# A fused attention and two expert layers in float32: scores of units 8 to 31 from split queries and keys, products with V in one burst

## The chip, the cores and the metric

The kernel runs on one core of a Trainium2 chip. The metric is the device time of one execution in microseconds (us), as the median of several runs. Five engines work side by side, each through its own list of instructions in order: TensorE (PE) for matrix products, VectorE (DVE), ScalarE (ACT), GpSimd (POOL), and SyncE (SP), which here issues nearly all DMAs. PEld is TensorE's loading of the stationary operand.

## The reference

Three layers follow one another: attention with a threshold on the scores, a layer `x -> (h - tanh h) @ w_out`, and a top-1 mixture of eight experts. Only the first is touched.

```python
def _attn_ref(q, k, v, tau):              # (4, 8, 576, 64) each
    scale = 1.0 / np.sqrt(q.shape[-1])
    scores = scale * np.matmul(q, k.transpose(0, 1, 3, 2))
    thresh = np.max(scores, axis=-1, keepdims=True) - tau
    scores = np.where(scores >= thresh, scores, -1000000000.0)
    scores = scores - np.max(scores, axis=-1, keepdims=True)
    attn = np.exp(scores)
    attn = attn / (np.sum(attn, axis=-1, keepdims=True) + 1e-09)
    return np.matmul(attn, v).astype(np.float32)
...
    x = attn_out.transpose(0, 2, 1, 3).reshape(B * S, H * D)      # 2304 x 512
    h = x @ w_in;  x = (h - np.tanh(h)) @ w_out                   # 512 -> 2048 -> 512
    ...                                                           # then top-1 of 8 experts, 512 -> 1024 -> 512
```

## The kernel before

**Stages.** Part A holds attention and, between its instructions, the first steps of the second layer on those chunks of 256 tokens whose attention is done (33 steps in all, `step`: 24 products `ph` of 256 columns at L606 and 12 products `x` of 512 columns at L640 each). Part B does the rest of that layer and the routing, and the last part the experts. Parts B and after are the same before and after the change, and the same 33 steps stand in part A.

**Units.** Attention is cut into 32 units: four batches, two halves of the queries, four pairs of heads (`units`). A unit of the first half has 2 x 128 queries in each of two heads, thus 4 score tiles of 128 queries by 576 keys; one of the second half has 5, the fifth a merged tile with the last 64 queries of both heads. That makes 144 tiles, 16 of them merged.

**A tile's way.** `scores_full` (L948) multiplies queries and keys in plain float32. The contraction over the head's 64 numbers fills half of the array's rows, so the two halves of the keys (288 each) stand on partitions 0 to 63 and 64 to 127 and run as two row tiles side by side: two calls of 288 columns, which the trace shows as four matmuls (`x4`, form 64*128); a merged tile has four calls and eight matmuls (form 64*64). DVE takes the tile out of PSUM with its row minimum of the negated scores (L963, `em`, `mx`), ACT does the exponential (L966, `e`), POOL or ACT the threshold (`tb`), DVE the masked product with the row sum (L976). PE turns the tile in four transposes (`turn`, L1013, `pt`), and ACT copies it to `eth`; the last 64 keys go through L1040 to `elh`.

**Products with V.** `pairs_` (L1058) multiplies by V in plain float32, each head in one half of the array's columns (form 128*64). Its eight calls for key tiles 0 to 3 (`x16` in the trace) are one scheduled piece, its two for key tile 4 (`x4`) a second one. ACT copies the result to `xf`, DVE multiplies by the turned reciprocals (L1097 to L1101), and ACT or POOL round it to `xh` while POOL keeps the remainder `xl`.

**Split numbers.** Elsewhere a float32 number is held as a rounded part (type fp32r) and a remainder (`round_to` at L424 to L428, `rest` at L436 to L444), and a product is made of several passes with these parts. `prep_q`, `prep_k` and the function `scores` hold this form for queries and keys; before, no unit uses them, since `FULL, FULLV = 32, 32`.

**Order.** `Sched` sorts all pieces of parts A and on by a greedy simulation: each piece has an engine, a duration in ns written in the code (for example 700 for `scores_full`, 2200 and 550 for the pieces of `pairs_`), a due time, and buffers with a fixed number of copies. The program is emitted in that order, so a change of such a number reorders all engines.

## Time and profile before

| | before |
|---|---|
| median of 3 runs | 1003.67 us (1002.45 to 1005.86) |
| the profiled execution | 1005.48 us |
| its span, first to last instruction | 1003.7 us |
| granted TensorE clock, mean | 0.996 |
| PE busy | 980.5 us (98%) |
| DVE, ACT, POOL busy | 680.0, 534.6, 316.5 us |
| score matmuls (L954), 640 | 112.2 us |
| products with V (L1062, key tiles 0 to 3), 512 | 70.5 us |

Matmuls are pipelined, so the length of one in the trace holds its way through the array; how much of PE a group takes is read as the distance from its start to the start of the next group, where nothing waits between them. A line `x4` of a timeline is four matmuls in a row.

### The profile page before, as it was taken

To read this page: it belongs to the slowest core of one execution; us is meant where nothing else is said; L and a number is where in the kernel's file an instruction comes from. 1 tells how busy PE (TensorE), PEld (TensorE's weight loads), DVE (VectorE), ACT (ScalarE), POOL (GpSimd) and SP (SyncE) were. 2 spreads that over 40 slices of the span, in tenths; PEclk is the share of its full clock that TensorE was granted. 3 is DMA by queue.
4 is the path that set the end of the run, shared out by engine and by line. 5 is a ranking of instruction groups with operands and counts; after the bars stand their busy time and mean duration, and the time that the engine had idled before them with its cause. 6 is when DMAs were issued, how large, how long until landed. Compare 5 with 4: busy or idle time off the path is not lost.

```text
span 1003.7 us, 18221 instructions
## 1 busy us (share of the span) xinstructions
PE 980.5 (98%) x6559; PEld 785.1 (78%) x6559; DVE 680.0 (68%) x1733; ACT 534.6 (53%) x1130; POOL 316.5 (32%) x531
## 2 busy tenths in 40 slices
PE   6899999999999999999999999999999999999997
PEld 3556677667777767767889888888898988999996
DVE  5988888777667555555268986697556785656640
ACT  4887777777666655656354443444332442334431
POOL 2556665455364434433400110011102320212101
PEclk9999999999999999999999999999999999999999
DMA  5464534644463451442592842321705784556501
GB/s 196 142 230 162 201 121 168 232 150 158 155 221 138 171 186 56 151 162 76 198 357 85 278 153 85 106 105 56 270 22 179 249 271 156 174 165 194 178 5 41
DMA packets 44564, 160.64 MB, mean 160 GB/s; under 512 B 5630, under 2 KB 5630, under 8 KB 38576
## 3 DMA queue, kind: packets, MB, share of 16 engines
q1 hardware_dynamic: 40896, 148.95, 42.7%
q0 software_dynamic: 3424, 10.16, 3.0%
q8 instruction: 54, 0.88, 0.4%
q14 instruction: 46, 0.38, 0.1%
q10 hardware_dynamic: 144, 0.26, 0.1%
HBM read 124.22 MB, written 35.85 MB: 159 GB/s over the span
## 4 chain that ended last, share of the span: by engine, by line
PE 90%; DVE 5%; issue 2%; ACT 1%; POOL 1%; DMA 1%; POOLq 0%; DVEq 0%; ACTq 0%
PE ph L606 21%; PE x L640 20%; PE ph L1615 10%; PE sp L954 8%; PE pv L1062 8%; PE py L1648 7%; PE pt L1013 6%; PE py L1502 4%; DVE em L976 1%; PE ph L1252 1%; DVE em L963 1%; PE pv L1040 1%; PE pt L1547 1%; PE x L700 1%; DMA tau_t<-in_tau_dram 1%
## 5 line engine op out<-in xcount | busy, mean ns | idle before, releaser
L606 PE MATMUL ph<-xh,wi 128*128 128x256 f32 x1152 | 184.9, 289 | 0.2 <-DVE u L629 0.2
L640 PE MATMUL x<-wo,gh 128*128 128x512 f32 x576 | 170.8, 408 | 0.6 <-POOL gh L426 0.6
L606 PEld LDWEIGHTS ph<-xh,wi 128*128 128x128 f32 x1152 | 157.4, 189 | 16.1 <-issue 10.9
L976 DVE SCALAR_TENSOR_TENSOR em<-em,tb,e 128x576 f32<-128x576 f32 x144 | 128.5, 895 | 50.9 <-ACT e L966 26.3
L963 DVE TENSOR_SCALAR_CACHE_REDUCE em<-sp 128x576 f32<-128x576 f32 x144 | 108.5, 754 | 54.7 <-PE sp L954 44.1
L966 ACT ACTIVATE e<-em,mx 128x576 f32<-128x576 f32 x144 | 111.0, 772 | 55.5 <-DVE em L963 47.2
L954 PE MATMUL sp<-kst,qh 64*128 64x288 f32 (+1 forms) x640 | 112.2, 463 | 9.1 <-DMA qh<-in_q_dram 4.9
L640 PEld LDWEIGHTS x<-wo,gh 128*128 128x128 f32 x576 | 98.8, 189 | 24.8 <-issue 9.3
L426 POOL TENSOR_SCALAR gh<-u 128x512 fp32r<-128x512 f32 x52 | 41.4, 797 | 215.8 <-DVE u L629 163.6
L424 ACT ACTIVATE eth<-pt 128x512 f32<-128x512 f32 (+1 forms) x160 | 85.8, 549 | 35.6 <-PE pt L1013 32.9
L606 PE MATMUL ph<-xl,wi 128*128 128x256 f32 x576 | 96.0, 289 | 0.0
L640 PE MATMUL x<-wo,gl 128*128 128x512 f32 x288 | 93.4, 408 | 0.0
L619 ACT ACTIVATE u<-ph 128x512 f32<-128x512 f32 x72 | 42.9, 596 | 94.0 <-PE ph L606 88.0
L1013 PE MATMUL pt<-ident,em 128*128 128x128 f32 x576 | 88.7, 280 | 3.9 <-DVE em L976 3.0
L1013 PEld LDWEIGHTS pt<-ident,em 128*128 128x128 f32 x576 | 67.8, 143 | 26.4 <-issue 8.7
L606 PEld LDWEIGHTS ph<-xl,wi 128*128 128x128 f32 x576 | 79.0, 190 | 6.7 <-issue 6.5
L627 DVE SCALAR_TENSOR_TENSOR w<-w,u 128x512 f32<-128x512 f32 x72 | 50.8, 706 | 45.0 <-ACT w L623 44.9
L954 PEld LDWEIGHTS sp<-kst,qh 64*128 64x128 f32 (+1 forms) x640 | 43.3, 179 | 43.1 <-issue 14.9
L444 DVE TENSOR_TENSOR w<-wraw,w 128x512 fp32r<-128x512 f32 x98 | 66.3, 693 | 11.8 <-ACT w L424 10.4
L1062 PE MATMUL pv<-eth,vt 128*64 128x256 f32 (+1 forms) x512 | 70.5, 417 | 0.0
L1536 POOL DMA_INDIRECT rows<-x2f,gid x20 | 21.9, 1096 | 127.4 <-PE pt L1547 121.2
L974 POOL TENSOR_TENSOR tb<-mx,tau_t 128x1 f32<-128x1 f32 x96 | 32.5, 338 | 91.0 <-DVE em L963 78.2
(372 smaller groups left out, 1807.8 us busy)
## 6 DMA issues: line engine op xcount, KB each, us to landing
wraw<-in_w_dram SPq DMA_DIRECT2D x64, 512.0 KB, 4.2
wi<-wsv SPq DMA_DIRECT2D x17, 1024.0 KB, 4.9
wo<-wsv SPq DMA_DIRECT2D x17, 1024.0 KB, 5.0
craw<-in_w_in_dram SPq DMA_DIRECT2D x14, 512.0 KB, 3.9
craw<-in_w_out_dram SPq DMA_DIRECT2D x14, 512.0 KB, 3.9
kst<-in_k_dram SPq DMA_DIRECT2D x16, 432.0 KB, 4.9
wsv<-wi SPq DMA_DIRECT2D x6, 1024.0 KB, 6.5
wsv<-wo SPq DMA_DIRECT2D x6, 1024.0 KB, 4.5
```

The costliest lines, as they stand in the source:

```text
L424: return sc.add("ACT", act(n, psum), due, lambda: nc.scalar.activation(dst(), src(), AF.Copy), r, w)
L444: return sc.add(eng, dve(n, psum) + 5 if eng == "DVE" else pool_tt(n), due, lambda: e.tensor_tensor(out=dst(), in0=src(), in1=hi().bitcast ...
L606: nc.tensor.matmul(ph.t[:, j, :], wi.t[:, w_, cc * CH + j * P:cc * CH + (j + 1) * P], x_.t[:, cc, :], start=(n == 0 and cc == 0), stop=(n ...
L640: nc.tensor.matmul(x2b[c, half][t].t, g_.t[:, j, t * P:(t + 1) * P], wo.t[:, w_, j * DM:(j + 1) * DM], start=(first and n == 0 and j == 0) ...
L954: nc.tensor.matmul(sp.t[o:o + m_, kb_, 0:KB], qh.t[rows, c0:c0 + m_], kf[rows, j * KB:(j + 1) * KB], start=True, stop=True)
L963: sc.add("DVE", 665, d, lambda ev=ev, sp=sp, mx=mx: nc.vector.tensor_scalar(out=ev().rearrange("p (a b) -> p a b", a=2), in0=sp.t[:, :, 0: ...
L966: sc.add("ACT", 667, d + 800, lambda e=e, ev=ev, mx=mx: nc.scalar.activation(e.t, ev(), AF.Exp, bias=mx.t, scale=-1.0), [(em, h), mx], [e])
L976: sc.add("DVE", 729, d + TAU, lambda ev=ev, tb=tb, e=e, rs=rs, h=h: nc.vector.scalar_tensor_tensor(out=ev(), in0=ev(), scalar=tb.t, in1=e. ...
L1013: nc.tensor.matmul(pt.t[:, kt, :], em.t[:, c0:c0 + P], ident, is_transpose=True, start=(kt == 0), stop=(kt == 3))
L1062: nc.tensor.matmul(pvf()[h * D:(h + 1) * D], vb_.t.rearrange("p a b -> p (a b)")[:, k * D:(k + 1) * D], eth[h].t[:, kt, 0:n] if kt < 4 els ...
L1615: nc.tensor.matmul(ph.t[:, 0:cap], wx()[:, cc * P:(cc + 1) * P], x_.t[:, cc, 0:cap], start=(n == 0 and cc == 0), stop=(n == 2 and cc == 3))
L1648: nc.tensor.matmul(py[j].t[0:size[j]], x_(), wx(), start=(f == 0 and n == 0), stop=(f == 7 and n == 2))
```

## The change

For units 8 to 31 the scores come from split numbers in the full array. `prep_q` loads a unit's queries twice (partitions 0 to 63 and 64 to 127), ACT rounds them to `qh`, and POOL makes the remainder `ql` in two halves. `prep_k` does the same for the keys of a pair of heads: ACT rounds twice 576 columns, and DVE or POOL put the remainder on partitions 64 to 127 (12 pairs of heads, 24 remainders, 12 of them on DVE). A score tile is then four matmuls of 288 columns with 128 contraction rows (rounded keys and remainder stacked, times `qh`, then `ql`); a merged one is ten, six of 288, two of 224 and two of 64 columns. Units 0 to 7 keep `scores_full`. The products with V stay in plain float32, but the ten calls are one piece that waits for `elh` too. The durations written in the code become 880 for `scores_full` and 3080 or 2560 for the burst; a split tile has 528, a merged one 1110. V's tile shrinks from 128 to 64 columns a head and key tile, as half of it was unused.

```diff
-FULL, FULLV = 32, 32
+FULL = 8
...
-        v_ = vts[b, hp] = buf("kv", "vt", 4, [P, 10, P])
-        dma(due - 6000, lambda: nc.sync.dma_start(
-            v_.t.rearrange("p a b -> p (a b)")[:, 0:10 * D],
-            vv[b, hp].rearrange("p a b -> p (a b)")), (), [v_], 327680)
+        v_ = vts[b, hp] = buf("kv", "vt", 4, [P, 10, D])
+        dma(due - 6000, lambda: nc.sync.dma_start(v_.t, vv[b, hp]), (), [v_], 327680)
...
-        full, fullv = ui < FULL, ui < FULLV
+        full = ui < FULL
...
                 if full:
-                    sc.add("PE", 700, d - TAU // 2, scores_full, [qh, kb], [sp])
+                    sc.add("PE", 880, d - TAU // 2, scores_full, [qh, kb], [sp])
                 else:
                     sc.add("PE", 1110 if merged else 528, d - TAU // 2, scores, [qh, ql] + kr_, [sp])
...
-            sc.add("PE", 2200 if half else 1780, dl, lambda: pairs_(range(4)), [vb_] + eth, [pv])
-            sc.add("PE", 550 if half else 445, dl, lambda: pairs_((4,)), [vb_, elh], [pv])
...
+        sc.add("PE", 3080 if half else 2560, dl, lambda: pairs_(range(5)), [vb_, elh] + eth, [pv])
```

The rest of the diff takes out code that no unit reached before (the split form of V's products, `prep_v`, the constant `minus`).

Two places in the order, before and after. First PE in the burst of unit 16 (first half of batch 2), from the last calls of key tiles 0 to 3 on: `sp` are scores, `eth` and `elh` the turned weights of attention, `ph` the second layer. Before:

```order
L1062 MATMUL pv<-eth_2986,vt 64x256
L1062 MATMUL pv<-eth_3011,vt 64x256
L606 MATMUL ph<-xh,wi_2723 128x256 x4
L1062 MATMUL pv<-elh,vt 64x256 x2
L606 MATMUL ph<-xl,wi_2723 128x256 x4
L954 MATMUL sp<-kst,qh 128x288 x2
L606 MATMUL ph<-xh,wi_2723 128x256 x8
```

The same burst after the change:

```order
L1030 MATMUL pv<-eth_3166,vt 64x256
L1030 MATMUL pv<-eth_3229,vt 64x256
L1030 MATMUL pv<-elh,vt 64x256 x2
L928 MATMUL sp<-kst,qh 128x288
L928 MATMUL sp<-kst,ql 128x288
L928 MATMUL sp<-kst,qh 128x288
L928 MATMUL sp<-kst,ql 128x288
L604 MATMUL ph<-xl,wi_2850 128x256 x4
```

Key tile 4 now follows the other four at once, and the score tile is four calls in the array's full form, as the second layer's calls around it are.

Second, POOL while batch 1 is under way, from a masked threshold (`tb`) on. Before:

```order
L974 TENSOR_TENSOR tb<-mx,tau_t 128x1
L995 TENSOR_SCALAR rb<-blk,rs 128x128
L426 TENSOR_SCALAR gh<-u 128x512
L438 TENSOR_TENSOR gl<-u,gh 128x256
L974 TENSOR_TENSOR tb<-mx,tau_t 128x1
L438 TENSOR_TENSOR gl<-u,gh 128x256
```

After:

```order
L959 TENSOR_TENSOR tb<-mx,tau_t 128x1 x2
L980 TENSOR_SCALAR rb<-blk,rs 128x128
L973 TENSOR_SCALAR rs<-rs 128x2
L424 TENSOR_SCALAR gh<-u 128x512
L436 TENSOR_TENSOR gl<-u,gh 128x256 x2
L436 TENSOR_TENSOR kst<-kr,kst 64x288
L424 TENSOR_SCALAR xh<-xf 128x128
L973 TENSOR_SCALAR rs<-rs 128x2
L442 TENSOR_TENSOR xl<-xf,xh 128x128
L436 TENSOR_TENSOR ql<-qr,qh 128x256
```

Remainders of keys (`kst`) and queries (`ql`) now stand among the thresholds, the reciprocals (`rs`) and the second layer's remainders (`gl`).

## Rows read from the trace of the kernel before

**Rows 1.** Busy time in six stretches: length, PE, PEld, DVE, ACT, POOL, clock, DMA.

```profile
25.00:50.00 25.00, 21.83 (x147) 13.05 (x148) 24.76 (x65) 21.14 (x45) 12.62 (x22) 1.00 0.43 143
...
75.00:100.00 25.00, 25.00 (x171) 16.14 (x168) 21.18 (x54) 18.77 (x41) 15.34 (x28) 0.95 0.47 164
100.00:150.00 50.00, 48.76 (x330) 33.65 (x329) 41.38 (x100) 37.15 (x81) 32.09 (x52) 1.00 0.46 162
150.00:200.00 50.00, 50.00 (x348) 34.46 (x347) 40.57 (x98) 36.56 (x79) 26.73 (x50) 1.00 0.59 200
...
450.00:485.00 35.00, 35.00 (x242) 26.08 (x241) 16.75 (x41) 21.79 (x49) 14.52 (x31) 1.00 0.21 76
...
520.00:600.00 80.00, 79.36 (x554) 70.67 (x553) 69.49 (x178) 39.39 (x82) 9.28 (x9) 1.00 0.53 182
```

**Rows 2.** L1062 by itself: duration min/median/max in ns, first and last start.

```profile
L1062 PE MATMUL pv<-elh,vt x128: 379/432/484, 24.3 to 483.3; 128*64 128x256 f32 x64, 128*64 128x320 f32 x64
```

**Rows 3.** PE in order of time around a burst: start, length, line, operation, form.

```profile
220.21 0.64 PE L606 MATMUL ph<-xh,wi 128*128 128x256 f32 x4
220.78 0.76 PE L954 MATMUL sp<-kst,qh 64*128 64x288 f32 x4
221.47 2.37 PE L1062 MATMUL pv<-eth,vt 128*64 128x320 f32 x16
223.67 0.71 PE L1062 MATMUL pv<-elh,vt 128*64 128x320 f32 x4
224.31 0.74 PE L606 MATMUL ph<-xl,wi 128*128 128x256 f32 x4
224.97 0.76 PE L954 MATMUL sp<-kst,qh 64*128 64x288 f32 x4
225.66 0.66 PE L1013 MATMUL pt<-ident,em 128*128 128x128 f32 x4
226.07 1.21 PE L606 MATMUL ph<-xh,wi 128*128 128x256 f32 x8
```

**Rows 4.** PE in order of time around a merged score tile.

```profile
211.88 0.72 PE L954 MATMUL sp<-kst,qh 64*64 64x288 f32 x8
212.53 0.74 PE L606 MATMUL ph<-xh,wi 128*128 128x256 f32 x4
213.10 0.65 PE L606 MATMUL ph<-xl,wi 128*128 128x256 f32 x4
213.58 0.60 PE L1013 MATMUL pt<-ident,em 128*128 128x128 f32 x4
213.94 0.73 PE L606 MATMUL ph<-xh,wi 128*128 128x256 f32 x4
```

**Rows 5.** PE in order of time, unit 16: a burst cut in two.

```profile
235.77 1.95 PE L1062 MATMUL pv<-eth,vt 128*64 128x256 f32 x16
237.65 0.73 PE L606 MATMUL ph<-xh,wi 128*128 128x256 f32 x4
238.31 0.65 PE L1062 MATMUL pv<-elh,vt 128*64 128x256 f32 x4
```

**Rows 6.** PE in order of time in the experts: split products of 288 columns.

```profile
916.89 0.69 PE L1615 MATMUL ph<-xh,w 128*128 128x288 f32 x4
917.42 0.69 PE L1615 MATMUL ph<-xl,w 128*128 128x288 f32 x4
917.95 1.22 PE L1615 MATMUL ph<-xh,w 128*128 128x288 f32 x8
```

**Rows 7.** Groups by line: count, then busy us, mean ns, idle before.

```profile
L424 ACT ACTIVATE wi<-ct 128x512 fp32r<-128x512 f32 x12 | 7.5, 622 | 0.3 <-DVE ct L557 0.3
L444 DVE TENSOR_TENSOR w<-wraw,w 128x512 fp32r<-128x512 f32 x98 | 66.3, 693 | 11.8 <-ACT w L424 10.4
```

**Rows 8.** From 75 to 485 us, single lines: duration min/median/max in ns.

```profile
L438 POOL TENSOR_TENSOR gl<-u,gh x61: 720/738/1297, 76.4 to 484.7; 128x256 fp32r<-128x256 f32 x61
...
L976 DVE SCALAR_TENSOR_TENSOR em<-em,tb,e x118: 800/818/1367, 76.7 to 476.8; 128x576 f32<-128x576 f32 x118
```

More of the change, by code (lines that the diff above doesn't have):

```diff
@@ L345, in tile_main @@
     make_identity(nc, ident)
-    minus = const.tile([P, P], F32R, name="minus")
-    nc.vector.tensor_scalar(out=minus, in0=ident, scalar1=-1.0, scalar2=None, op0=ALU.mult)
     tau_t = const.tile([P, 1], F32, name="tau_t")
@@ L909, in attention @@
         n = 320 if half else 256
-        full, fullv = ui < FULL, ui < FULLV
+        full = ui < FULL
         kb, vb_ = kst[b, hp], vts[b, hp]
         qh, ql = qs
-        dt_ = F32 if fullv else F32R
-        eth = [buf("et", f"eth{h}", 1, [P, 4, 320], dt_) for h in range(2)]
-        elh = buf("et", "elh", 1, [P, 320], dt_)
-        if not fullv:
-            etl = [buf("et", f"etl{h}", 1, [P, 4, 320], F32R) for h in range(2)]
-            ell = buf("et", "ell", 1, [P, 320], F32R)
+        eth = [buf("et", f"eth{h}", 1, [P, 4, 320]) for h in range(2)]
+        elh = buf("et", "elh", 1, [P, 320])
         T0 = k0 * TAU
@@ L1024, in attention @@
                     hi = lambda hh=hh, cols=cols: eth[hh].t[:, :, cols]
-                    if fullv:
-                        round_to("p_h", 4 * wd, d + 400, hi, src, [pt], [(eth[hh], qt)], True)
-                        continue
                     round_to("p_h", 4 * wd, d + 400, hi, src, [pt], [(eth[hh], qt)], True)
-                    lo = lambda hh=hh, cols=cols: etl[hh].t[:, :, cols]
-                    if not merged and pick("p_x") == "Z":
-                        sc.add("PE", 231, d + 700, lambda pt=pt, hi=hi: nc.tensor.matmul(
-                            pt.t, minus, hi(), start=False, stop=True, skip_group_check=True), [(eth[hh], qt)], [pt])
-                        round_to("p_lz", 512, d + 900, lo, src, [pt], [(etl[hh], qt)], True)
-                        continue
-                    rest("p_l", 4 * wd, d + 900, lo, src, hi, [pt, (eth[hh], qt)], [(etl[hh], qt)], True)
             plist.append((em, qt, merged, d))
@@ L1045, in attention @@
             round_to("p_h2", D, dl + 500, lambda: elh.t[D:P, 256:320], lambda: plf()[D:P, 320:384], [pl], [elh], True)
-        if not fullv:
-            rest("p_l", n, dl + 900, lambda: ell.t[:, 0:n], lambda: plf()[:, 0:n], lambda: elh.t[:, 0:n],
-                 [pl, elh], [ell], True)
-        if half and not fullv:
-            rest("p_l", D, dl + 900, lambda: ell.t[D:P, 256:320], lambda: plf()[D:P, 320:384],
-                 lambda: elh.t[D:P, 256:320], [pl, elh], [ell], True)
         xf = buf("ep", "xf", 1, [P, 320])
@@ new lines, in attention, with pairs_ @@
+        pv = buf("ps_v", "pv", 1, [P, 4, P])
+        pvf = lambda: pv.t.rearrange("p a b -> p (a b)")[:, 0:n]
+        def pairs_(kts):
+            for kt in kts:
+                for h in range(2):
+                    k = 2 * kt + h
+                    nc.tensor.matmul(
+                        pvf()[h * D:(h + 1) * D], vb_.t[:, k, :],
+                        eth[h].t[:, kt, 0:n] if kt < 4 else elh.t[:, 0:n], start=(kt == 0), stop=(kt == 4))
+        sc.add("PE", 3080 if half else 2560, dl, lambda: pairs_(range(5)), [vb_, elh] + eth, [pv])
@@ L1151, in tile_main @@
                 raw_k(0, k, (starts[k] - 4) * TAU)
[L1152 to L1153 removed]
+                raw_v(0, k, (starts[k] + 1.5) * TAU)
             qnext = raw_q(0, T0 - 4 * TAU)
@@ L1159, in tile_main @@
             qnext = prep_q(*units[ui + 1], T0 + 0.5 * TAU)
-        if half == 0 and (b or not FULLV):
-            (raw_v if ui < FULLV else prep_v)(b, hp, T0 + 1.5 * TAU)
+        if half == 0 and b:
+            raw_v(b, hp, T0 + 1.5 * TAU)
         if b and half == 0:
@@ L1169, in tile_main @@
             prep_k(b, hp, (starts[ui + 4] - 4) * TAU)
-        if ui < 4 and 0 < FULLV < 8:
-            prep_v(b, hp, (starts[ui + 4] - 2) * TAU)
         sc.kind = "moe"
```

44 lines of the change are left out of this document (2 added, 42 removed), and 3 rows, old and new, of the table ENGINES.

## The prediction

> **What bounds the kernel now.** I read first the table of busy time by stretch. Attention and the second layer's first steps share part A, whose last product with V starts at 483.3 us [rows 2]. From 150 to 200 us PE is busy 50.00 of 50.00 us, from 450 to 485 again 35.00 of 35.00, while DVE is at 0.81 and then 0.48 of the time [rows 1]. Only earlier is it otherwise: from 25 to 50 us DVE is busy 24.76 of 25 and PE 21.83. So in part A, once the second layer can fill the gaps, the end is set by how much PE has to do; every us taken from PE's list there moves all that follows, until DVE or ACT come up to it. The clock is full in these stretches but one (0.95 from 75 to 100 us) [rows 1].
>
> A busy PE says nothing of how long its pieces are, so I next read PE's list in order of time, by the distance from a group's start to the next group's start. In [rows 3] a plain score tile takes 221.47 - 220.78 = 0.69 us. The `ph` group ahead of it takes 220.78 - 220.21 = 0.57, where a `ph` group with split products on both sides, or transposes behind it, takes 213.58 - 213.10 = 0.48 [rows 4]: going over from the full array to row or column tiles costs 0.09. The `ph` group behind a score tile takes 213.10 - 212.53 = 0.57 [rows 4], so the way back costs 0.09 too. Both are paid at one group in 224.97 - 224.31 = 0.66, which comes from column tiles and goes to row tiles [rows 3]. These changes are a hidden half of the cost of the scores: a tile between full-array work costs 0.69 + 0.09 + 0.09 = 0.87.
>
> **The change part by part.**
>
> *The ordinary score tile of units 8 to 31* (96 tiles): 0.69 before. After, it is four split matmuls of 288 columns in the full array, and the experts run just these: four in 917.42 - 916.89 = 0.53 us, weights loaded anew for each [rows 6]. Saved: 96 x 0.16 = 15.4 us.
>
> *The merged tile* (12 of them): before, 212.53 - 211.88 = 0.65 [rows 4]. After, six matmuls of 288 columns at 0.53/4 = 0.13 make 0.80, and two of 224 at no more than 0.48/4 = 0.12 [rows 4] make 0.24, rather 0.21 as they have fewer columns. For those of 64 columns no row exists; their price lies between 64/288 of 0.13, which is 0.03, and the 0.10 that one transpose of 128 columns takes, 226.07 - 225.66 = 0.41 for four behind a score tile [rows 3]. I take 0.10, as the transpose too has 128 weight columns to load. Sum 1.21, lost: 12 x 0.56 = 6.7 us (at the lower end 5.0).
>
> *The changes of form.* I counted them in the order of the two programs, up to the end of attention: from full array to tiles 138 times before and 54 after, back 139 and 55, directly between scores' row tiles and V's column tiles 51 and 11. Saved: 84 pairs at 0.09 + 0.08 (some of the ways back lead to transposes, which pay only 0.06: 0.41 for four behind a score tile [rows 3] against 213.94 - 213.58 = 0.36 behind `ph` [rows 4]) = 14.3 us; and 40 direct changes at something between 0 and 0.10, for which I take 0.07, 2.8 us. In this count lies the burst's part: before, 15 of the 32 bursts are cut in two by other work, as in [rows 5], where `ph` stands between and takes 238.31 - 237.65 = 0.66 with both changes in it; after, none is. The burst's own calls stay as they are (2.20 and 0.64 us in [rows 3]). It now waits for `elh` as well; behind it wait PE's next scores, and DVE for these, but in 17 of 32 bursts the second piece followed directly before, so that `elh` was there in time. I cost that wait at nothing while the second layer's steps stand ahead of the burst; without that cover it is at most the 0.4 us or so of one copy, for 15 bursts 6 us, which I keep for the range.
>
> *Sum on PE:* 15.4 - 6.7 + 14.3 + 2.8 = 25.8 us less.
>
> *What other engines get.* ACT: 24 roundings of queries (512 or 704 columns) and 24 of keys (576), at 622 ns for 512 columns [rows 7] some 0.62 to 0.8 each: 33 us. POOL: 48 half remainders of queries and 24 of keys; 256 columns take 738 ns [rows 8], 352 in proportion 1.0: 61 us. DVE: 12 remainders at 0.70 [rows 7], 8 us. They are off PE's path as long as they come half a unit early; in the order the second half of `ql` stands at least some hundred allocations ahead of its first score, where a unit has about two hundred. SP issues 36 more DMAs, for the halves that are loaded twice; bytes hardly change, and transfers have a share of 0.46 to 0.59 [rows 1]. The load is nevertheless near the top for a stretch: from 100 to 200 us DVE was busy 82 of 100 us, ACT 74, POOL 59 [rows 1]. With PE's work there some 9 us shorter and a fifth of the added work in it, DVE comes to 0.92, ACT to 0.88, POOL to about 0.8.
>
> *What that costs PE* no row shows for this mix, so I bound it. Below: nothing, as from 150 to 200 us with DVE at 0.81. Above: 3.17 of 25 us, or 13%, as from 25 to 50 us with DVE at 0.99 and little to fill the gaps. Between lie 1.24 of 50 us, 2.5% (100 to 150 us, DVE 0.83), and 0.64 of 80 us, 0.8%, with DVE at 0.87 and ample split products [rows 1]. I take 2.5% for the first 100 us of the changed part and 0.8% for the other 285: 2.5 + 2.3 = 4.8 us.
>
> *A rule that speaks against this.* DVE's masked product takes 818 ns in the middle and 1367 at most, POOL's remainder 738 and 1297 [rows 8]: now and then one stands still for about the length of the other, mostly not. The Trainium skill (SBUF — State Buffer, SBUF: two separate sides) calls the port pair of VectorE and GpSimd an exclusive lock, held for the whole instruction, for VectorE's instructions with two inputs from SBUF among others. The longest durations here agree with that; the medians, 18 ns above the shortest, say that it strikes seldom. By the rows it is thus a few us in DVE's gaps and nothing in the sum; what it would be if it struck each time is the last rival.
>
> *Total:* 25.8 - 4.8 = 21.0 us less. The profiled execution of before took 1005.48 us with a span of 1003.7, so it would be 984.5 there; it lies 1.8 above the median of 1003.67, against which I forecast **982.7 us**.
>
> **The rivals.**
>
> *DVE and ACT take over until batch 2.* For: DVE at 0.92, and in-order engines lose at each late input; PE's planned durations now are near the true ones, which leaves others less slack. Against: units 8 to 12 had filled gaps at 0.83, and the second layer's steps lie several units behind, so PE has other work. Price: 13% on the first 100 us and 2.5% on the rest, 13 + 7.1 = 20.1; 25.8 - 20.1 = 5.7 less, 998 us.
>
> *The split queries come late: slower.* Each unit's first tile needs the load, one rounding on ACT and two remainders on POOL, with POOL's list of thresholds and `gl` ahead of them, and only two copies of `ql`. If PE stood still for a whole conversion at each of 24 units, 0.7 + 2 x 0.87 = 2.4 us, that is 58 us against 25.8 saved: 1036 us. It decides from 25.8/24 = 1.1 us per unit on. For: POOL would have to be at about 0.8. Against: the order places it half a unit ahead, some 7 us.
>
> *The forms change as before.* If the split tiles between transposes (plain float32) pay as much at each change as row tiles do, the 17.1 us for changes are not had: 25.8 - 17.1 - 4.8 = 3.9 less, 999.8 us. Against: `ph` groups stand between transposes and split products all over part A, and in [rows 4] a change from `ph` to transposes takes nothing (0.48).
>
> *DVE and POOL stop each other: slower.* If each of the 72 new POOL operations kept a DVE operation waiting for its whole length, as the longest of [rows 8] do, and each such wait reached PE, that would be 61 us against 25.8: 1039 us. It decides from 25.8/72 = 0.36 us each on. Against: the medians of [rows 8], and DVE's idle 18 of each 100 us from 100 to 200. This is the lock of the page named above, taken at its word.
>
> **How the numbers follow.** Forecast, 976 to 991 us (25.8 with the merged tile at its lower end and no idle, down to 13 less where `elh` and the port cost 8): 0.71. Better than that: 0.03. DVE and ACT, 991 to 1000: 0.14. The forms: 0.05. Late queries: 0.05. The port: 0.02. The range of 975 to 995 takes in the forecast and half of the first rival, with 0.2 left out. About 0.3%, 3 us, is what a measurement of this kernel can tell from no change. Faster by more: 0.88; within it 0.05, the weak ends of the two milder rivals; slower 0.07.
>
> **What would show it.** Right: a split tile takes 0.53 to the next start, the `ph` group ahead of it 0.48; the last product with V starts some 20 us earlier than 483.3; PE's idle time between 75 us and that point stays under 8 us, and the parts behind keep their length. The first rival shows as PE idle on DVE's row minimum or masked product between 100 and 220 us; the second as PE's scores waiting for POOL's `ql` or `kst`; the third as split tiles of 0.7. The forecast is wrong if PE's list isn't the bound once it is shorter, or if part B doesn't start earlier by what part A saves.

## The result, and the profile after

The changed kernel takes **995.21 us** (median of four runs, 992.77 to 995.42), beside 1004.32 us for the kernel before (1002.45 to 1005.86): a ratio of 0.9905, 95% interval 0.9881 to 0.9928. That is faster by 9.1 us where 21.0 were forecast, and just outside the range, whose upper end was 995.

| | before | after |
|---|---|---|
| profiled execution, its span | 1005.48, 1003.7 us | 995.42, 993.5 us |
| mean granted clock | 0.996 | 0.995 |
| PE busy | 980.5 us | 960.0 us |
| DVE, ACT, POOL busy | 680.0, 534.6, 316.5 us | 710.5, 559.2, 400.8 us |
| V burst of unit 7 starts | 105.49 us | 117.27 us |
| V burst of unit 31 starts | 480.84 us | 472.87 us |

First the table of busy time by stretch (length, PE, PEld, DVE, ACT, POOL, clock, DMA), the rows that answer to [rows 1] and the stretch from 50 to 75 us beside them:

```profile
25.00:50.00 25.00, 19.97 (x125) 11.52 (x123) 21.89 (x56) 17.98 (x37) 9.86 (x20) 0.93 0.37 126
50.00:75.00 25.00, 20.40 (x134) 12.94 (x136) 21.45 (x52) 18.47 (x39) 14.23 (x22) 0.93 0.63 206
75.00:100.00 25.00, 23.29 (x157) 14.52 (x153) 23.24 (x51) 21.01 (x45) 18.39 (x31) 1.00 0.53 165
100.00:150.00 50.00, 45.92 (x333) 35.16 (x333) 46.58 (x107) 40.08 (x88) 42.84 (x63) 1.00 0.60 187
150.00:200.00 50.00, 50.00 (x366) 41.85 (x365) 46.83 (x105) 42.29 (x93) 43.26 (x64) 1.00 0.51 171
200.00:300.00 100.00, 98.95 (x714) 83.75 (x714) 85.02 (x183) 78.45 (x170) 81.13 (x120) 1.00 0.58 183
450.00:485.00 35.00, 35.00 (x241) 29.29 (x240) 14.92 (x44) 17.66 (x43) 15.95 (x30) 1.00 0.33 118
```

From 150 us on PE is as full as before, with one us missing from 200 to 300. What is new stands above that: from 25 to 150 us PE is idle 5.03 + 4.60 + 1.71 + 4.08 = 15.4 us. Before it was 3.17 + 0 + 1.24 by [rows 1], and 2.34 more by the row of before that was not shown:

```profile
50.00:75.00 25.00, 22.66 (x167) 14.55 (x163) 22.27 (x60) 20.43 (x45) 13.29 (x27) 0.98 0.67 225
```

together 6.75 us. Of the 8.7 us more, 5.8 lie ahead of 100 us, where no split score has started yet (the first one does at 110.0 us; the first conversion, a rounding of keys on ACT, starts at 63.3). The granted clock was lower there too: 0.93 from 25 to 75 us, thus 3.5 us of full-speed time at most, where before lost 0.5 and 1.25 (0.98 and 0.95 from 50 to 100 us).

Next PE in order of time around split tiles, a merged one and a burst (start, length, line, operation, form), which answers to [rows 3, 4]:

```profile
115.35 0.63 PE L604 MATMUL ph<-xl,wi 128*128 128x256 f32 x4
115.82 0.64 PE L604 MATMUL ph<-xh,wi 128*128 128x256 f32 x4
...
160.73 0.29 PE L928 MATMUL sp<-kst,qh 128*128 128x288 f32 x1
160.86 0.29 PE L928 MATMUL sp<-kst,ql 128*128 128x288 f32 x1
160.99 0.29 PE L928 MATMUL sp<-kst,qh 128*128 128x288 f32 x1
161.12 0.29 PE L928 MATMUL sp<-kst,ql 128*128 128x288 f32 x1
161.25 0.38 PE L1015 MATMUL pv<-ident,em 128*128 128x128 f32 x2
...
162.42 0.63 PE L638 MATMUL x<-wo,gh 128*128 128x512 f32 x2
162.89 0.29 PE L928 MATMUL sp<-kst,qh 128*128 128x288 f32 x1
...
225.75 2.38 PE L1030 MATMUL pv<-eth,vt 128*64 128x320 f32 x16
227.96 0.71 PE L1030 MATMUL pv<-elh,vt 128*64 128x320 f32 x4
228.60 0.40 PE L928 MATMUL sp<-kst,qh 128*128 128x288 f32 x1
...
284.02 0.38 PE L928 MATMUL sp<-kst,qh 128*128 128x288 f32 x1
...
285.26 0.71 PE L638 MATMUL x<-wo,gh 128*128 128x512 f32 x2
```

A split tile takes 161.25 - 160.73 = 0.52 us, a group of `ph` in the same form 0.47, a merged tile 285.26 - 284.02 = 1.24, and two `x` calls ahead of a split tile 0.47, with nothing paid for a change of form. The burst keeps its 2.21 and 0.64. These pieces came out as the prediction priced them; their sum over part A is looked at below.

Then where attention stands, by the start of a unit's burst. Unit 7, the last with plain scores, and unit 31 (a group is cut at the edge of its view, hence `x2`), in after:

```profile
117.27 2.37 PE L1030 MATMUL pv<-eth,vt 128*64 128x320 f32 x16 [0.82 <-ACT elh L422]
...
472.87 0.49 PE L1030 MATMUL pv<-eth,vt 128*64 128x320 f32 x2
```

and in before:

```profile
105.49 0.49 PE L1062 MATMUL pv<-eth,vt 128*64 128x320 f32 x2
...
480.84 0.49 PE L1062 MATMUL pv<-eth,vt 128*64 128x320 f32 x2
```

Unit 7, none of whose scores has changed, is 11.8 us late, and unit 31 is 8.0 us early. Such a mark is to be corrected for the second layer's calls that stand ahead of it, which I counted in the trace: at unit 7 after has 72 `ph` calls behind it where before has 48, at 0.1185 us each, so 2.8 us of the 11.8 are work brought forward and **8.9 are lost**. At unit 31 it has ten `x` more (0.2325 each), so it is 10.3 early. Between the two marks after is thus 8.9 + 10.3 = **19.2 us shorter**. (Attention's own calls ahead of a mark are not corrected. At unit 7 three split tiles stand ahead where before has three plain ones, and one group of four transposes is missing, so the true loss is up to 0.9 larger.) (The last product with V starts at 475.4 instead of 483.3 [rows 2]; the ten `x` calls that are done by then make the rest 518.1 us long instead of 520.4.)

PE up to the first mark and between the two (length, PE, clock, DMA), in after:

```profile
0.00:117.27 117.27, 95.69 (x592) 0.97 0.58 183
117.27:472.87 355.60, 352.47 (x2542) 1.00 0.51 165
```

and in before:

```profile
0.00:105.49 105.49, 92.08 (x572) 0.98 0.53 183
105.49:480.84 375.35, 374.11 (x2530) 1.00 0.45 156
```

Ahead of unit 7's burst PE is idle 21.6 us in after and 13.4 in before: 8.2 more, so the loss is idle time on PE, with at most 1.75 us from the lower clock. Between the marks the clock is full and PE idles 3.1 against 1.2 us. As after is 19.2 us shorter there in spite of 1.9 us more idle time, PE's list between the marks became some 21 us shorter.

What the engines wait for ahead of unit 7. The view of waits (engine, line, what it waited for, us in total, times, longest), PE from 20 to 75 us, after:

```profile
PE sp L939 <- DVE em L948: 5.5, 8, 1.6
PE pt L998 <- DVE em L961: 2.3, 3, 1.0
PE pv L1015 <- DVE em L961: 1.0, 2, 0.5
```

before:

```profile
PE sp L954 <- DVE em L963: 2.9, 4, 1.2
PE pv L1040 <- DVE em L976: 1.0, 3, 0.5
```

and DVE from 25 to 75 us, after:

```profile
DVE em L961 <- ACT e L951: 3.4, 4, 1.0
DVE em L948 <- PE sp L939: 1.5, 3, 1.0
DVE rs L976 <- POOL rs L973: 1.2, 2, 0.9
```

before:

```profile
DVE em L963 <- PE sp L954: 1.6, 2, 1.0
DVE em L963 <- PE pv L1040: 1.3, 1, 1.3
DVE rs L991 <- POOL rs L988: 0.5, 1, 0.5
DVE em L976 <- ACT e L966: 0.2, 1, 0.2
```

PE waits for DVE, and DVE, which before was busy 24.76 of 25 us [rows 1], now itself waits for ACT's exponential: in the first units the four engines hand one tile round, and more of the handing over comes late. Up to 63.3 us no split number is touched, and from there to 75 us five conversions are. Yet from 25 to 63.3 us PE already idles 7.0 us in after and 3.6 in before. Up to there three things can differ: the order in which the same pieces stand, the joined bursts, and the granted clock.

That this can be so at all lies in how the order is made. The planner goes over all pieces of parts A and on in turn forwards and backwards, and takes the priorities of a pass from the times of the pass before; so a shorter piece in unit 20, or another written duration, changes what stands first in unit 1. The core of it:

```python
            order, start, end = self.greedy(prio)
            ...
                _, s_, e_ = self.greedy([-e for e in end], True)
                prio = [-e for e in e_]
```

### The profile page after: what moved, and what is told of

It is laid out like the page before. It is cut to its first block, busy times and chain, and to the rows that moved or that the text cites. A ratio compares the mean times of both kernels' runs of the same rounds, so it can differ in the third digit from the quotient of the medians.

```text
span 993.5 us, 18537 instructions
## 1 busy us (share of the span) xinstructions
PE 960.0 (97%) x6583; PEld 820.0 (83%) x6583; DVE 710.5 (72%) x1744; ACT 559.2 (56%) x1178; POOL 400.8 (40%) x603
## 4 chain that ended last, share of the span: by engine, by line
PE 80%; DVE 9%; issue 3%; DMA 2%; ACT 2%; POOL 2%; POOLq 0%; SPq 0%; DVEq 0%; ACTq 0%
PE x L638 18%; PE ph L604 18%; PE ph L1556 10%; PE py L1589 7%; PE pv L1030 6%; PE sp L928 6%; PE pt L998 4%; PE py L1443 4%; DVE em L961 2%; DVE em L948 2%; PE ph L1193 1%; DVE ct L552 1%; PE pt L1488 1%; DVE ct L555 1%; PE x L698 1%
## 5 line engine op out<-in xcount | busy, mean ns | idle before, releaser
L604 PE MATMUL ph<-xh,wi 128*128 128x256 f32 x1152 | 181.6, 287 | 0.0
L961 DVE SCALAR_TENSOR_TENSOR em<-em,tb,e 128x576 f32<-128x576 f32 x144 | 140.8, 980 | 32.6 <-ACT e L951 18.9
L638 PEld LDWEIGHTS x<-wo,gh 128*128 128x128 f32 x576 | 98.9, 189 | 17.5 <-issue 1.8
L422 ACT ACTIVATE eth<-pt 128x512 f32<-128x512 f32 (+1 forms) x160 | 85.4, 548 | 25.8 <-PE pt L998 25.5
L998 PEld LDWEIGHTS pt<-ident,em 128*128 128x128 f32 x576 | 69.4, 144 | 20.6 <-DVE em L961 10.7
L442 DVE TENSOR_TENSOR w<-wraw,w 128x512 fp32r<-128x512 f32 x98 | 66.2, 692 | 11.8 <-ACT w L422 10.4
L928 PE MATMUL sp<-kst,qh 128*128 128x288 f32 (+2 forms) x252 | 72.9, 308 | 1.7 <-DVE em L948 1.5
L928 PE MATMUL sp<-kst,ql 128*128 128x288 f32 (+2 forms) x252 | 68.0, 293 | 0.0
L1561 ACT ACTIVATE hh<-ph 128x384 fp32r<-128x384 f32 (+4 forms) x56 | 24.7, 442 | 62.5 <-PE ph L1556 62.4
```

The source lines that it names most:

```text
L422: return sc.add("ACT", act(n, psum), due, lambda: nc.scalar.activation(dst(), src(), AF.Copy), r, w)
L442: return sc.add(eng, dve(n, psum) + 5 if eng == "DVE" else pool_tt(n), due, lambda: e.tensor_tensor(out=dst(), in0=src(), in1=hi().bitcast ...
L604: nc.tensor.matmul(ph.t[:, j, :], wi.t[:, w_, cc * CH + j * P:cc * CH + (j + 1) * P], x_.t[:, cc, :], start=(n == 0 and cc == 0), stop=(n ...
L638: nc.tensor.matmul(x2b[c, half][t].t, g_.t[:, j, t * P:(t + 1) * P], wo.t[:, w_, j * DM:(j + 1) * DM], start=(first and n == 0 and j == 0) ...
L928: nc.tensor.matmul(sp.t[:, kb_, o:o + w], q_.t[:, q0:q0 + P], kb.t[:, hh, c0:c0 + w], start=(i == 0), stop=(i == len(todo) - 1),)
L961: sc.add("DVE", 729, d + TAU, lambda ev=ev, tb=tb, e=e, rs=rs, h=h: nc.vector.scalar_tensor_tensor(out=ev(), in0=ev(), scalar=tb.t, in1=e. ...
```

## Experiments

Three theories: the **load** of the new conversions on DVE, POOL and ACT takes the gain; the **order** of the first units does (by the new durations, by the joined burst, or because everything is planned anew); or the **roundings on ACT** hold up the burst. In the table, "unit 7" and "unit 31" are the starts of their bursts in the profile of each run, less those of before, corrected as above for the second layer's calls that stand ahead. The ratio is to executions of the kernel before taken beside that run, whose median differs a little from row to row. The marks are of one profiled execution; that of pin100 is its fastest (996.22 us).

| run | ratio to before (95%) | median us | unit 7 | unit 31 |
|---|---|---|---|---|
| the changed kernel | 0.9905 (0.9881 to 0.9928) | 995.2 | +8.9 | -10.3 |
| burst_only | 1.0054 (1.0034 to 1.0075) | 1009.7 | +3.7 | +3.1 |
| scores_only | 0.9871 (0.9855 to 0.9888) | 992.7 | +8.4 | -11.6 |
| zero_rest | 0.9854 (0.9837 to 0.9870) | 990.6 | +6.5 | -15.6 |
| full16 | 0.9918 (0.9902 to 0.9935) | 997.2 | +8.5 | -8.8 |
| dur_only | 1.0091 (1.0060 to 1.0122) | 1012.7 | +4.1 | +6.1 |
| burst_old | 1.0020 (1.0001 to 1.0039) | 1007.0 | +4.0 | +2.2 |
| scores16 | 0.9931 (0.9912 to 0.9950) | 997.7 | +5.4 | -8.0 |
| late_all | 0.9902 (0.9873 to 0.9930) | 994.1 | +4.7 | -12.9 |
| before_margin | 1.0006 (0.9994 to 1.0017) | 1004.5 | -1.8 | -1.7 |
| before_r12 | 1.0007 (0.9996 to 1.0017) | 1004.2 | -0.1 | -0.7 |
| after_r8 | 0.9905 (0.9879 to 0.9931) | 993.4 | +8.4 | -13.3 |
| after_r19 | 0.9933 (0.9916 to 0.9949) | 995.8 | +11.0 | -9.4 |
| pin | 0.9999 (0.9982 to 1.0016) | 1002.9 | +17.5 | -1.2 |
| pin100 | 0.9968 (0.9956 to 0.9979) | 1000.5 | +5.8 | -9.6 |
| pin_s100 | 0.9878 (0.9859 to 0.9898) | 991.7 | +1.6 | -13.7 |
| pin_s100_zero | 0.9887 (0.9857 to 0.9917) | 990.0 | +1.7 | -15.3 |
| pin_s16 | 0.9884 (0.9867 to 0.9900) | 992.7 | +1.3 | -12.5 |
| pin_dur | 1.0062 (1.0045 to 1.0078) | 1009.8 | -3.6 | +2.3 |

**The two halves of the change.** The burst and the new durations without split scores, and the split scores without them:

```diff
-FULL = 8
+FULL = 32
```

> The changed kernel with unsplit scores in all 32 units: the single burst of V and the new planned durations alone. PE's list of part A is 1 us shorter than before by the distances read in the trace of before. If the loss of about 15 us against the sum on PE comes from the remainders of queries and keys on POOL and DVE (theory 1), this kernel takes about what before takes, 1001 to 1005 us, and PE's work done by 150 us is as before. If the new order of the first units causes it (theory 2), part of the loss is here too: 1007 to 1013 us, and PE idles more than before between 25 and 75 us.

```diff
-FULL, FULLV = 32, 32
+FULL, FULLV = 8, 32
```

> The kernel before with split scores in units 8 to 31 and nothing else: V in two pieces, the old planned durations. PE's list of part A is 27 us shorter than before. Theory 1 (load on POOL and DVE): about 995 us like the changed kernel, the loss is the same. Theory 2 (new order of the first units): 980 to 987 us.

The first is slower than before although its list on PE is a us shorter. The second is faster than the changed kernel. That is what the order theory expected of the first; the second lies between the two theories. So the burst and the durations are no part of the gain, and the split scores alone get 12 to 13 us. By the prediction's own prices, with the changes of form counted in this run's trace, they take 15.4 - 6.7 + 77 x 0.17 + 35 x 0.07 = 24.2 us off PE's list: about half of it doesn't come out here either, and unit 7 is 8.4 us late.

**The remainders.** The changed kernel with every remainder of queries and keys replaced by a memset of the same tile:

```diff
+        zero = cls in ("q_l", "k_l")
...
+                if zero:
+                    return nc.gpsimd.memset(a[:, cut].bitcast(F32), 0.0)
...
```

> The changed kernel in its own order, but each remainder of queries and keys is set to zero by a memset (no inputs) in place of the subtraction: this leaves out the low parts of the scores. ACT's roundings, the DMAs, PE's list and the order stay. Theory 1: POOL's and DVE's operations no longer stop each other more than before, and most of the loss comes back: 982 to 987 us. Theory 2: it stays at 993 to 996 us. If ACT's roundings or the single staging buffer of the keys are the cause (theory 3), it stays at 993 to 996 us too.

5 us less than the changed kernel (0.9905 to 0.9854), which lies between what the load theory and the other two expected. So the remainders do cost time, but not the whole of what is missing. DVE's masked product shows one way in which they act. Line by itself from 75 to 485 us (duration min/median/max in ns), in after and in this run:

```profile
L961 DVE SCALAR_TENSOR_TENSOR em<-em,tb,e x120: 796/878/1458, 77.9 to 467.7; 128x576 f32<-128x576 f32 x120
```

```profile
L965 DVE SCALAR_TENSOR_TENSOR em<-em,tb,e x120: 799/819/1378, 76.8 to 462.4; 128x576 f32<-128x576 f32 x120
```

Before, the median was 818 [rows 8]. But most of these durations lie near 0.82 us and the others spread from 0.9 to 1.46, and a median tells little of such a mixture. The mean of all 144 does (busy us, mean ns): before, after, this run, and split scores without the other edits:

```profile
L976 DVE SCALAR_TENSOR_TENSOR em<-em,tb,e 128x576 f32<-128x576 f32 x144 | 128.5, 895 | 50.9 <-ACT e L966 26.3
L961 DVE SCALAR_TENSOR_TENSOR em<-em,tb,e 128x576 f32<-128x576 f32 x144 | 140.8, 980 | 32.6 <-ACT e L951 18.9
L965 DVE SCALAR_TENSOR_TENSOR em<-em,tb,e 128x576 f32<-128x576 f32 x144 | 132.5, 923 | 34.7 <-ACT e L955 18.8
L976 DVE SCALAR_TENSOR_TENSOR em<-em,tb,e 128x576 f32<-128x576 f32 x144 | 138.3, 964 | 38.9 <-ACT e L966 20.1
```

Counted in the traces, 31 of 144 took over 0.95 us before, 59 after, 38 with the memsets and 51 in scores_only, where the median from 75 to 485 us is only 830. So with 72 more POOL operations 28 more masked products are a few tenths of a us longer, together 12.3 us of DVE's time, of which 8.3 are gone with the memsets. The Trainium skill (SBUF — State Buffer, SBUF: two separate sides) calls the port pair of these two engines an exclusive lock; the longer group agrees with it. It is the prediction's last rival in kind, but far from its size: 12 us on DVE, which has gaps, instead of 61 on PE. Unit 7 comes 2.4 us earlier in this run and is still 6.5 late: the remainders explain a part of what holds up the first units, and not the larger one.

**Split scores from unit 16 on.** The first split score starts at 223.8 us in scores16 (223.1 in full16), the first conversion, a rounding of keys on ACT, at 173.7 in both. The first is the changed kernel, the second the kernel before with split scores alone:

```diff
-FULL = 8
+FULL = 16
```

> The changed kernel with split scores from unit 16 on only. PE's list of part A is 18 us shorter than before, 8 longer than in the changed kernel, and the remainders fall where DVE and POOL have more idle time. Theory 1: the loss shrinks to some 3 to 5 us, so 988 to 991 us, faster than the changed kernel. Theory 2: the loss of 11 us in the first units stays, 997 to 1001 us.

```diff
-FULL, FULLV = 32, 32
+FULL, FULLV = 16, 32
```

> The kernel before with split scores from unit 16 on alone, all old durations, burst in two pieces. PE's list is some 17 us shorter, all of it behind 230 us, where other engines have room; before that nothing differs but what the greedy order makes of it. If the loss in the changed kernel comes from the order of units 0 to 7 by the new durations and the joined burst, this gains nearly all of it: 987 to 990 us. If it comes from the conversions' load wherever they stand, it gains 10 to 12 us, 992 to 994.

The first run came out as the order theory expected. It has the changed kernel's burst and durations, and its unit 7 is as late as there, 8.5 us against 8.9, though no rounding and no remainder stands ahead of it (PE idles 19.6 us up to there, 6.2 more than before, at a granted clock of 0.94). So neither is needed for that lateness. The second run was slower than either theory expected. It has all old durations and the old burst, its list is 64 x 0.16 - 8 x 0.56 + 51 x 0.17 + 25 x 0.07 = 16.2 us shorter, and from unit 7 to unit 31 it gains 5.4 + 8.0 = 13.4 of them. Yet unit 7 is 5.4 us late, ahead of anything split, by work that is the same.

**Durations alone, burst alone, both late.**

```diff
-                    sc.add("PE", 700, d - TAU // 2, scores_full, [qh, kb], [sp])
+                    sc.add("PE", 880, d - TAU // 2, scores_full, [qh, kb], [sp])
...
-            sc.add("PE", 2200 if half else 1780, dl, lambda: pairs_(range(4)), [vb_] + eth, [pv])
-            sc.add("PE", 550 if half else 445, dl, lambda: pairs_((4,)), [vb_, elh], [pv])
+            sc.add("PE", 2464 if half else 2048, dl, lambda: pairs_(range(4)), [vb_] + eth, [pv])
+            sc.add("PE", 616 if half else 512, dl, lambda: pairs_((4,)), [vb_, elh], [pv])
```

> The kernel before with nothing changed but the durations written for the greedy order: 880 for a plain score tile and 3080 or 2560 for the burst (its two pieces stay apart). The work is the same instruction for instruction. Joined burst and new durations together were 4.8 us slower than before. If the durations are to blame (they order the first units, in which every tile is plain), this is 4 to 6 us slower than before as well, 1007.5 to 1010 us, with PE idle some 2 us more between 25 and 75 us. If the joined burst is to blame, it is within 2 us of before.

```diff
-            sc.add("PE", 2200 if half else 1780, dl, lambda: pairs_(range(4)), [vb_] + eth, [pv])
-            sc.add("PE", 550 if half else 445, dl, lambda: pairs_((4,)), [vb_, elh], [pv])
+            sc.add("PE", 2750 if half else 2225, dl, lambda: pairs_(range(5)), [vb_, elh] + eth, [pv])
```

> The kernel before with the burst as one piece that waits for elh, and the old durations (700; 2750 or 2225, the sum of the two pieces). The counterpart of the run above: 1007 to 1010 us if PE's wait for the last key tile costs the 5 us, within 2 us of before (less 1 us of list) if the durations do.

```diff
-                    sc.add("PE", 880, d - TAU // 2, scores_full, [qh, kb], [sp])
+                    sc.add("PE", 700, d - TAU // 2, scores_full, [qh, kb], [sp])
...
-        sc.add("PE", 3080 if half else 2560, dl, lambda: pairs_(range(5)), [vb_, elh] + eth, [pv])
+        if full:
+            sc.add("PE", 2200 if half else 1780, dl, lambda: pairs_(range(4)), [vb_] + eth, [pv])
+            sc.add("PE", 550 if half else 445, dl, lambda: pairs_((4,)), [vb_, elh], [pv])
+        else:
+            sc.add("PE", 3080 if half else 2560, dl, lambda: pairs_(range(5)), [vb_, elh] + eth, [pv])
```

> The changed kernel, but for units 0 to 7 the burst in two pieces and the old durations (700; 2200 and 550, or 1780 and 445), so that what is planned for these units is as before; split scores and joined burst from unit 8 on. If the order of the first units is the larger part of the loss: 986 to 990 us. If the joined burst or the conversions of units 8 to 12 are: 991 to 995.

The same instructions with other numbers written beside them cost 8 us and more (0.9% of the time), beyond what was expected: a duration in the code is as real a change as an instruction. In the profiled execution of dur_only PE idles 17.1 us up to unit 7's burst, 3.7 more than before, at the same granted clock (0.98). The joined burst alone costs 2 us, with an interval that nearly reaches none; that is at the edge between what was expected of either cause. The two don't add up (both together cost 5). The old numbers and the old burst for the first units (late_all) bring unit 7 from 8.9 to 4.7 us late, but the time hardly moves: that is the range for the joined burst or the conversions of units 8 to 12, and not the order theory's.

**Is it one unlucky order?** The planner keeps one of 25 passes; these runs take other ones, or change the pause that it puts between pieces:

```diff
-MARGIN = 60
+MARGIN = 80
```

> The kernel before with one number of the greedy order changed that is no duration: the 60 ns that are added between two pieces when the order is made become 80. The same work in a slightly different order on all engines. If the time of part A hangs on which order the first units happen to get (theory 2), this differs from before by several us, likelier slower (1008 to 1012 us), and PE has done less of its list by 75 us. If the order is of little weight, 1003 to 1007 us.

```diff
+PICK = 12
...
-            if best is None or span < best[0]:
+            pick_ = any(o.kind == "att" for o in self.ops)
+            if best is None or (r == PICK if pick_ else span < best[0]):
```

> The kernel before in another order of its own (sweep 12). If the order of the kernel before was a good draw among its kind, this is 3 to 8 us slower, 1007 to 1012 us; if orders count for little where PE's list is the bound, 1002 to 1006.

The same edit in the changed kernel, with 8 and then 19:

> The changed kernel in another of the 25 orders that its planner makes by going over the work forwards and backwards in turn (it keeps one; this is the one of sweep 8). Same instructions, same durations. Order theory: the time of part A depends on which order comes out, so this differs from the changed kernel by 3 us or more, 990 to 1003 us. Load theory (remainders and roundings near PE's pace): within 3 us, 993 to 998.

> The changed kernel in a third order (sweep 19). Order theory: again 3 us or more away from one of the other two. Load theory: 993 to 998 us.

No. Three orders of the kernel before lie within 1 us, three of the changed kernel within 2.4 (2.8 by the ratios), and in all three of these unit 7 is 8 to 11 us late. So it is no single unlucky draw; the order theory had expected 3 us or more between the draws, and that was wrong, as was the expectation that before had drawn well. The clock has a larger part in the two other orders: up to unit 7's burst it was 0.94 and 0.93, up to 7.0 and 8.3 us of full-speed time, beside 0.97 and 3.5 in the changed kernel; PE idles 21.1 and 20.6 us there, as in the changed kernel.

**Keeping the order of the first units.** A table gives every piece that also stands in before the place on its engine that it has there, up to some 75 us (pin) or 115 us (the others); what is new goes between, and behind it the program's own order holds:

```diff
+            for o in sorted((o for o in self.ops if o.key in PIN), key=lambda o: PIN[o.key]):
+                if o.eng in last:
+                    o.starts.add(last[o.eng])
+                last[o.eng] = o
...
```

> The changed kernel, in which every piece of work that also stands in the kernel before, up to the softmax of unit 4 or so (to about 75 us), keeps the place on its engine that it has in the kernel before; the joined burst stands where the burst's second piece stood. All later pieces follow the changed kernel's own order. Nothing is added or left out. Theory 1 (the load that the remainders put on POOL and DVE): those remainders come later, so the time stays at 993 to 997 us. Theory 2 (the loss sits in the order that the new durations give to the first units): PE has done by 75 us as much of its list as before, 4 to 7 us more than in the changed kernel, and the end comes 4 to 7 us earlier, 988 to 991 us. Theory 3 (roundings on ACT): 993 to 997.

> The same with the order of the kernel before kept for the shared work to about 115 us, through most of units 0 to 7; the conversions of the queries and keys of unit 8 and later stand where the changed kernel's own rule puts them between. Theory 2: 984 to 989 us, with PE's work done by 100 us within 3 us of that of before. Theory 1: the remainders now fall among work that was placed without them, so the stalls come back later, 992 to 998. If the first run gains 5 us and this one nothing more, the order counts to about 75 us alone.

> The kernel before with the split scores of units 8 to 31 alone (burst in two pieces, all old durations kept), and the order of before kept for the shared work to about 115 us. Unpinned it took 0.987 of the time of before. Theory 2: 3 to 6 us less than unpinned, 986 to 990 us. Theory 1: 991 to 995, as unpinned, since the same conversions are done.

> The kernel with split scores alone and the first 115 us in the order of the kernel before, its remainders of queries and keys replaced by a memset of zero of the same tile (the low parts of the scores are left out). Without that replacement 991.7 us. In the changed kernel's own order the remainders cost 4.6 us. Load theory: the same 4 to 6 us or more here, 985 to 988. If the loss at 100 to 125 us here comes from the place of the conversions among kept work and not from their length, 990 to 992.

> Split scores from unit 16 on alone, old durations, burst in two pieces (997.7 us as it came out), with the order of the kernel before kept for all work of the first 115 us. No conversion of queries or keys stands in that stretch. Order theory: the 7.8 us that the unpinned run had lost by 150 us come back, 988 to 991 us, which is nearly the whole 16 us that PE's list is shorter. If the early loss is only moved behind the kept stretch: 995 to 999 us.

> The kernel before with the new durations (880; 3080 and 2560) and the same work (1012.7 us as it came out), with the order of the kernel before kept for the first 115 us. Order theory: what the durations cost lies in the first units, so 1003 to 1006 us. If it lies in the whole of part A or is moved behind the kept stretch: 1009 to 1013 us.

Where no conversion stands in the kept stretch, this helps: scores16 goes from 0.9931 to 0.9884, the intervals just apart, and unit 7 from 5.4 us late to 1.3; dur_only goes from 1.0091 to 1.0062, which the intervals don't part. Stretches of pin_s16, then of scores16:

```profile
25.00:75.00 50.00, 45.07 (x317) 27.95 (x316) 46.11 (x121) 40.38 (x87) 26.69 (x50) 1.00 0.55 173
75.00:150.00 75.00, 69.17 (x472) 46.17 (x473) 60.46 (x147) 55.80 (x119) 41.17 (x76) 1.00 0.50 170
```

```profile
25.00:75.00 50.00, 43.18 (x298) 24.76 (x294) 43.67 (x112) 37.97 (x80) 23.27 (x41) 1.00 0.47 154
75.00:150.00 75.00, 70.11 (x462) 46.02 (x462) 60.77 (x149) 55.40 (x122) 46.21 (x80) 0.98 0.53 182
```

From 25 to 75 us PE gets 1.9 us and DVE 2.4 back; from 75 to 150 us PE is still idle 5.8 of 75, where before it was idle 1.24, though no conversion stands there. So the kept order brings back a part of before's timing, and not all of it.

Where conversions stand there, it doesn't. In pin_s100 unit 7 is nearly on time, 1.6 us late where scores_only was 8.4; but from unit 7 to 31 it gains 1.6 + 13.7 = 15.3 us, scores_only 8.4 + 11.6 = 20.0, and the times can't be told apart. From 75 to 150 us in pin_s100:

```profile
75.00:150.00 75.00, 67.06 (x473) 49.22 (x472) 68.26 (x150) 60.58 (x129) 59.65 (x90) 1.00 0.52 169
```

PE idles 7.9 us, with DVE at 0.91 and POOL at 0.80. Taking the remainders out of this order brought nothing that can be told (0.9878 and 0.9887), against the load theory. With the joined burst the kept order was worse than the program's own, 1000.5 and 1002.9 us, and slower than any of the three theories expected. In none of the five runs for which the order theory named a time did it come out there. In pin TensorE's clock fell too. The stretch, and PE inside it:

```profile
75.00:150.00 75.00, 65.94 (x411) 45.59 (x408) 60.40 (x139) 56.35 (x120) 52.13 (x83) 0.88 0.56 177
```

```profile
93.40 0.66 PE L1080 MATMUL pt<-ident,em 128*128 128x128 f32 x4 [0.95 <-DVE em L1043]
94.53 0.72 PE L1021 MATMUL sp<-kst,qh 64*64 64x288 f32 x8 [0.47 <-DVE em L1030]
97.54 1.12 PE L1080 MATMUL pt<-ident,em 128*128 128x128 f32 x4 [2.30 <-DVE em L1043]
...
102.26 3.78 PE L720 MATMUL x<-wo,gh 128*128 128x512 f32 x8
105.84 0.65 PE L1080 MATMUL pt<-ident,em 128*128 128x128 f32 x4
```

Behind waits of 0.95, 0.47 and 2.30 us for DVE the transposes at 97.54 us take 1.12 us in all, where four took 0.66 at 93.40; eight `x` calls take 105.84 - 102.26 = 3.58, where eight at 0.235 make 1.88; and the transposes at 105.84 take 0.65 again. Between the two the granted clock was at the lower of its levels, 1.2 instead of 2.4 GHz. So a gap on PE can cost more than its length. The four runs of the changed kernel had a mean clock of 0.992 to 0.995, those of before 0.993 to 0.999 with most at 0.996 or more: at some 4 in 1000 lower, that is about 4 us of full-speed time in 995, an upper bound for its part in the loss. Between the two profiled executions it is 1.75 us at most.

## Why the prediction was wrong

**The pieces: right; their sum (25.8 us): some 3 too large.** Split tile 0.52 (forecast 0.53), merged 1.24 (1.21), nothing paid for a change of form at split tiles, the burst's calls unchanged. But between the marks, where 93 plain and 12 merged tiles, 82 pairs of changes and 32 direct ones fall, the prices make 14.9 - 6.7 + 13.9 + 2.2 = 24.3 us, and PE's list became some 21 shorter. As the tiles' own distances hold, the changes of form are likely priced too high; no run here singles them out.

**What fuller engines cost PE in the changed part (4.8 us): some 3 too large.** From 100 to 200 us PE idles 4.08 us and from 200 to 300 1.05, but 1.24 from 100 to 150 were there before and are no new cost. Between the marks it is 3.1 us against 1.2, thus 1.9 more. DVE came to 0.93 from 100 to 200 us (forecast 0.92), POOL to 0.86 (0.8), ACT to 0.82 (0.88). From unit 7 to unit 31 the changed kernel gains 19.2 us, 8.4 + 13.3 = 21.7 and 11.0 + 9.4 = 20.4 in its other two orders. The sum said 21.0. That it comes out so near is in part luck: two errors of about 3 us cancel.

**The failed step: the bound was carried over to the stretch ahead of the change, which was priced at nothing.** "Once the second layer can fill the gaps, the end is set by how much PE has to do" holds from 150 us on. Up to unit 7 PE has gaps in both kernels (13.4 us of idle time before, 21.6 after), and the sum spoke only of the first 100 us of the changed part. By unit 7 the changed kernel has lost 8.9 us (8.4 and 11.0 in the other orders), for the most part as more idle time on PE (8.2 us), and that is the difference: 19.2 - 8.9 = 10.3 against the profiled gain of 1005.48 - 995.42 = 10.06. The list of signs had the same hole: PE's idle time was to be watched from 75 us on, and there it kept the bound (1.71 + 4.08 + 1.05 = 6.8 us, none from 300 us on, under 8), while the last product with V started 7.9 us earlier and not some 20.

**What made unit 7 late.** Shown: it needs no new work, as full16, scores16 and dur_only have none by then and are 8.5, 5.4 and 4.1 us late; in dur_only, where every instruction is as before, only the order is left. All three orders of the changed kernel have it; and where no new work stands between, keeping the old order takes it away (scores16 to 1.3, dur_only to 3.6 early). So the larger part of unit 7's lateness comes with the order that the planner makes of the same pieces when durations, joins or later units change. Shown too: the remainders cost some 5 us of the end in the changed kernel, 2.4 of them by unit 7; and up to 1.75 us in the profiled execution can be the lower clock. Not shown: that an earlier unit 7 gives the time back. It did in pin_s16 (some 5 us less than scores16). It did not in late_all (4.7 late instead of 8.9, the same time), in pin_s100, which gets less out of units 8 to 31, with DVE at 0.91 of the time from 75 to 150 us, or in pin_dur, which is 3.6 us early at unit 7 and 2.3 late at unit 31. Not settled: why the new orders are all worse here and those of before are not, and why the kept order doesn't help with the joined burst in it. The waits say only that tiles are handed over later between DVE, ACT and PE. The cause behind the failed step is thus open in part.

**The wait for `elh`** was costed at nothing: it is 1.2 us in two bursts in the whole of part A, 0.82 of it at unit 7, and joining the burst cost 2 us by itself. That lies within the 6 us kept for it, and undoes most of the 2.8 us that fewer direct changes of form were to bring.

**The rivals.** DVE and ACT taking over (998 us) is near in time and wrong in place: it wanted 13% of PE idle from unit 8 on, and PE idles 4.08 of 100 us from 100 to 200. Late split queries: in part A PE waits for no `ql`, and for `kst` only at its first load. The forms changing as before: refuted by the rows of the tiles. DVE and POOL stopping each other: 28 more masked products are long, which fits it, but for 12 us of DVE's time in all. The prediction had read from the median that this strikes seldom; by the mean before, 895 ns, and the 31 of 144 over 0.95 us, one in five was long already.

**A better version.** The split scores with the old burst and the old durations (scores_only, 0.9871) are 2.6 us ahead of the changed kernel (0.9905) in the medians, with intervals that still overlap, so this is likely and not shown; the kept order adds nothing that can be told (0.9878). By itself the joined burst with its durations costs 5 us (burst_only), so the edit that looked like PE's tidier half is the one to leave out first.

## What to carry to other kernels

Where a program's order is planned as a whole, a local change is two changes: its own work, and a new order everywhere, the stretches with gaps above all. Price the first by rows, and give the second a term of its own; a run with nothing but the new durations shows whether it matters. Then read the time by marks inside the program (here the bursts of the last unchanged unit and of the last changed one, corrected for other work brought forward), since the total had mixed a sum that came out nearly right with a stretch that the sum had not looked at. And where durations fall into two groups, read their mean or count the long ones; the median hides them.

## What the runs showed of the hardware

TensorE's clock fell to its lower level behind waits of PE for DVE of 0.95, 0.47 and 2.30 us (pin), and in the changed kernel, from 25 to 75 us at 0.93, with no wait of PE longer than 1.6 us; in pin it stayed there for several us of dense work (eight `x` calls in 3.58 us). Runs of one order then spread by 7 us (996.22 to 1003.26 in pin100), where those of before spread by 4. And the masked product on DVE went from 895 ns in the mean to 980 when POOL had 72 more two-operand operations, and to 923 when these were memsets: 31, 59 and 38 of 144 took over 0.95 us.
